# Two quads' sums joined between VectorE's block transpositions, their rows in another order as the output weights are loaded

## The chip, the cores and the metric

The kernel runs on one core of a Trainium2 chip. A core has a matrix engine (TensorE, in the profile PE, with its weight loads as PEld), a vector engine (VectorE, DVE), an engine for functions such as exp (ScalarE, ACT), a general engine (GpSimd, POOL) and an engine that issues transfers (SyncE, SP). Every engine has a queue of its own, works through it in order, and waits on semaphores of the others. All transfers of this kernel are issued from SP's queue, and 16 DMA engines carry them.

The metric is the device time of one execution in microseconds (us); lower is better. A difference of some 0.2% is about what can be told from no change.

## What is computed

Four attention layers stand one behind the other on x of 2048 tokens by 512 features. Layers 0 and 2 (kind A) look back over a window of 256 tokens; layers 1 and 3 (kind B) look at all tokens, with no causal mask. Both kinds have 32 heads of 16 features, with their own weights, and each kind's weights serve two layers.

```python
def _A_ref(x, wqkv, wo):
    B, S, D = x.shape
    H = 32; Dh = D // H; W = 256
    qkv = (x @ wqkv).reshape(B, S, 3, H, Dh).transpose(2, 0, 3, 1, 4)
    q, k, v = qkv[0], qkv[1], qkv[2]
    scores = jnp.einsum("bhqd,bhkd->bhqk", q, k) * (Dh ** -0.5)
    mask = (idx[:, None] - idx[None, :] >= 0) & (idx[:, None] - idx[None, :] < W)
    scores = jnp.where(mask[None, None], scores, -1e9)
    p = _softmax(scores, axis=-1)
    o = jnp.einsum("bhqk,bhkd->bhqd", p, v)
    return o.transpose(0, 2, 1, 3).reshape(B, S, D) @ wo
...
x = x + _A_ref(_layernorm(x, axis=-1), A_wqkv, A_wo)
x = x + _B_ref(_layernorm(x, axis=-1), B_wqkv, B_wo)
x = x + _A_ref(_layernorm(x, axis=-1), A_wqkv, A_wo)
x = x + _B_ref(_layernorm(x, axis=-1), B_wqkv, B_wo)
```

## The kernel before

**Tiles and loops.** The 2048 queries go in four chunks of 512 (index c). The 32 heads go in eight quads of four heads (index qd); two quads make one of four head tiles of 128 features (t = qd // 2, and u = qd % 2 is the half). For each chunk and quad TensorE makes scores (`exps`, lines 693 to 706), ScalarE takes exp of them (line 705), in the windowed layers GpSimd zeroes the edges of the window (lines 768 and 771), and TensorE multiplies with the values into one PSUM bank `a` (line 745 in the full layers, 778 in the windowed ones). Head h of the quad stands in partitions 32h to 32h+16: 16 rows of sums and one row with the sum of the weights.

**The epilogue of a quad (lines 664 to 690).** VectorE transposes the bank in blocks of 32 by 32 (line 671), so that queries are in the partitions and the 32 rows of a head side by side; takes the sums of weights, records their least and their total (674, 675), makes reciprocals (677, 678) and multiplies the 16 sums (679). It transposes back (681) into `o`, where half of the 32 rows of each head mean nothing. It then splits `o` into a float16 part (683) and the float16 rest (684, on GpSimd in layers 1 and 3 except for the last quad), into the tile `hl`. Four transfers (line 688) take the 16 good rows of each head from `hl` into the packed tile `O[l, c, t]`, 64u + 16h + d being the row. `o` and `hl` have one buffer each, O has five.

**The output projection.** `wo` (627) and, in layer 3, `wo_part` (646) multiply O with the output weights on TensorE (lines 415 and 418, as "oh" in the profile), scale columns with `gcol`, add to x and write it back to a scratch tensor. `ONR[l, c, t]` holds the modelled time at which O is taken to be there: 9 us after the epilogue is written out.

**Weights.** `prep` does the preparation of one matrix beside other work: `load_w` (270) loads it in one transfer of 1 MB with row k\*128 + p in partition p, `maxima` takes the columns' maxima, `scales` (303) makes powers of two from them, and `parts` (325) makes two float16 parts, which go to a scratch tensor `wd` (347) and are loaded from there by each projection (383, 385). The scales of the values' columns (`upv`) are multiplied onto the rows of the output weights (line 280).

**What sets the order.** TensorE's order is written out by hand. While a layer's attention runs, `Side` puts pieces of "works" (projections K, Q, VV for the next chunk or layer, and OO, the output projection) between its steps; a piece comes when a modelled clock says that what it needs is there (`DONE`, `ONR`) and by a share of the steps. A planner orders the other engines' queues; in the full layers the epilogue's first transposition is put ahead. SP's queue carries, in one order, the loads of queries and keys of each quad (`qt`, lines 718 and 731; `kt`, 722, 732 and 734), of weights, of x, the transposing transfers of the normalised x (`xc<-xh`, 476), the writes of projections, and the four transfers of line 688.

**The end.** The last thing is the part of layer 3's output projection that uses the last two quads; only then x goes out.

Of the kernel before, what the change touches and what calls it, by code (L numbers as in the profile page):

```python
# [9 lines left out]
F32 = mybir.dt.float32  # L10
BF16 = mybir.dt.bfloat16
F16 = mybir.dt.float16
# [3 lines left out]
ALU = mybir.AluOpType  # L16
AX = mybir.AxisListType

S, D, H, DH, WIN = 2048, 512, 32, 16, 256
P = 128  # L20
# [3 lines left out]
NHT = H // HT  # L24
QC = 512
NQ = S // QC
EPS = 1e-5
NQD = H // 4
# [5 lines left out]
EB, XB, XNB, WB, VB, OB = 6, 4, 4, 2, 3, 5  # L34
# [141 lines left out]
def interleave_kernel(tc, *args):  # L176
    nc = tc.nc
    with tc.tile_pool(name="flag", bufs=1) as fp:
        flag = fp.tile([1, 1], I32, name="flag")
        fast_path(tc, flag, *args)  # L180
        good = nc.values_load(flag, min_val=0, max_val=P)
        with tc.If(good < P):
            general_path(tc, *args)
# [3 lines left out]
def fast_path(ctx, tc, flag, a_x, a_wqkv, a_wo, b_wqkv, b_wo, out):  # L187
# [3 lines left out]
    nc = tc.nc  # L191
    pool = lambda name, bufs, **k: ctx.enter_context(tc.tile_pool(name=name, bufs=bufs, **k))
    cp = pool("const", 1)
    wp = pool("wts", 2)
    vp = pool("work", 2)
# [9 lines left out]
    mats = {(ty, s): layers[ty][1][:, s * D:(s + 1) * D] if s < 3 else layers[ty][2]  # L205
            for ty in range(2) for s in range(4)}

    XC, XN, V, O, KM, PH = {}, {}, {}, {}, {}, {"free": 0.0}
    CM, DN, DC, WT, ST, pend = {}, {}, {}, {}, {}, []

    clock, DONE, XNR, ONR = [0.0], {}, {}, {}
# [11 lines left out]
    acc = [ps_c.tile([P, QC], F32, name=f"acc{i}") for i in range(2)]  # L223
    turn = {"s": 0, "bank": 0}
    ident = cp.tile([P, P], F32, name="ident")
    onesf = cp.tile([P, P], F32, name="onesf")
    ones = cp.tile([P, QC], F16, name="ones")
    hsum = cp.tile([P, 32], BF16, name="hsum")
    es = cp.tile([P, 2, 2, NHT], F32, name="es")
    upv = cp.tile([P, 2, NHT], F32, name="upv")  # L230
# [10 lines left out]
    rows = lambda t: t.rearrange("p (h r) n -> (p h) r n", r=R)  # L241

    make_identity(nc, ident)
    nc.gpsimd.memset(onesf, 1.0)
    nc.gpsimd.memset(ones, 1.0)
    nc.gpsimd.memset(zeros, 0.0)
# [22 lines left out]

    def load_w(ty, s):  # L270
        raw = wp.tile([P, NC, D], F32, name=f"wr{ty}_{s}", tag="vf", bufs=NQ)
        nc.sync.dma_start(raw, mats[ty, s].rearrange("(k p) f -> p k f", p=P))
        return raw

    def maxima(ty, s, raw):
# [27 lines left out]
    def scales(ty, s):  # L303

        n = f"{ty}_{s}"
        cm = CM.pop((ty, s))
        up = es[:, ty, s, :] if s < 2 else upv[:, ty, :] if s == 2 else vp.tile([P, NHT], F32, name=f"wu{n}", tag="wc", bufs=8)
        dn = vp.tile([P, NHT], F32, name=f"wn{n}", tag="wc", bufs=8)
        nc.vector.tensor_scalar(up.bitcast(I32), cm.bitcast(I32), 0x7F800000, None, op0=ALU.bitwise_and)
        nc.vector.tensor_scalar(dn.bitcast(I32), up.bitcast(I32), -1, 0x7F000000, op0=ALU.mult, op1=ALU.add)  # L310
        DC[ty, s] = dn
        for v, name in ((up, "u"), (dn, "d"))[0 if s == 3 else 1:]:
            dg = vp.tile([P, NHT, P], F32, name=f"{name}g{n}", tag="oe")
            nc.vector.tensor_tensor(dg, ident[:, None, :].broadcast_to([P, NHT, P]),
                                    v[:, :, None].broadcast_to([P, NHT, P]), ALU.mult)
            yield
            pb = bank()
            nc.tensor.matmul(pb, onesf, dg.rearrange("p t f -> p (t f)"), start=True, stop=True)
            if name == "u":
                nc.vector.tensor_copy(gcol[ty], pb)  # L320
            else:
                DN[ty, s] = vp.tile([P, D], F32, name=f"wd{n}", tag="dn", bufs=2)
                nc.scalar.activation(DN[ty, s], pb, AF.Copy)

    def parts(ty, s, raw, act):

        dnb = DN.pop((ty, s))
        w = wp.tile([P, NC, 2, D], F16, name=f"w{ty}_{s}", tag="vf", bufs=NQ)
        hi, lo = w[:, :, 0, :], w[:, :, 1, :]
        mul = lambda k: (nc.vector if act else nc.gpsimd).tensor_tensor(raw[:, k, :], raw[:, k, :], dnb, ALU.mult)  # L330
        cast = lambda k: nc.scalar.activation(hi[:, k, :], raw[:, k, :], AF.Copy)
        rest = lambda k: nc.gpsimd.tensor_tensor(lo[:, k, :], raw[:, k, :], hi[:, k, :], ALU.subtract)
        if act:
            for k in range(NC):
                mul(k), cast(k), rest(k)
                yield
            WT[ty, s] = w
        else:

            for f, n, pause in (mul, 1, 2), (cast, 2, 1), (rest, 1, 0):  # L340
                for k in range(NC):
                    f(k)
                    if k % n == n - 1:
                        yield
                for _ in range(pause):
                    yield
        nc.sync.dma_start(wd[ty, s], w)

    def prep(ty, s):
        raw = load_w(ty, s)  # L350
        yield wait(14)
        for _ in maxima(ty, s, raw):
            yield wait(2)
        yield -spent(1.0)
        for _ in scales(ty, s):
            yield wait(4)
        if (ty, s) == (1, 0):
            share(1)
        yield -spent(0.5)
        for _ in parts(ty, s, raw, False):  # L360
            yield wait(2)
# [34 lines left out]
    def bank():  # L396

        if PH["full"]:
            return acc[1]
        turn["bank"] += 1  # L400
        if turn["bank"] % 2 and not PH["win"]:
            return ps_s.tile([P, 2, QC], F32, name=f"bs{turn['bank']}", tag="s")[:, 0, :]
        return PH["pool"].tile([P, QC], F32, name=f"b{turn['bank']}", tag="b")
# [260 lines left out]
    def epilogue(l, c, qd, a):  # L664


        n = f"{l}_{c}_{qd}"
        t, u = divmod(qd, 2)
        ot = vp.tile([P, QC // 32, 32], F32, name=f"ot{n}", tag="oe")
        with tc.high_priority(HEAD_START if l % 2 else 0):  # L670
            nc.vector.transpose(ot.rearrange("p b r -> p (b r)"), a)  # L671
        den = ot[:, :, DH]

        nc.vector.tensor_tensor(lmin, lmin, den, ALU.min)
        nc.vector.tensor_add(lsum, lsum, den)
        r = vp.tile([P, QC // 32], F32, name=f"r{n}", tag="r")
        nc.vector.tensor_scalar_max(r, den, L_MIN)
        nc.vector.reciprocal(r, r)
        nc.vector.tensor_tensor(ot[:, :, :DH], ot[:, :, :DH], r[:, :, None].broadcast_to([P, QC // 32, DH]), ALU.mult)
        o = vp.tile([P, QC], F32, name=f"o{n}", tag="o", bufs=1)  # L680
        nc.vector.transpose(o, ot.rearrange("p b r -> p (b r)"))
        hl = vp.tile([P, 2, QC], F16, name=f"hl{n}", tag="hl", bufs=1)
        nc.vector.tensor_copy(hl[:, 0], o)  # L683
        (nc.gpsimd if l % 2 and (l, c, qd) != (3, NQ - 1, NQD - 1) else nc.vector).tensor_tensor(hl[:, 1], o, hl[:, 0], ALU.subtract)  # L684
        if u == 0:
            O[l, c, t] = wp.tile([P, 2, QC], F16, name=f"oh{n}", tag="ohl", bufs=OB)
        for h in range(4):
            nc.sync.dma_start(O[l, c, t][64 * u + DH * h:64 * u + DH * h + DH], hl[32 * h:32 * h + DH])  # L688
        if u:
            ONR[l, c, t] = clock[0] + 9  # L690


    def exps(name, kt, qt, pr, pieces):
# [248 lines left out]
    def attention(l, works):  # L942
# [5 lines left out]
        for t in range(NHT if l == 3 else 1):  # L948
            for c in range(NQ):
# [10 lines left out]
                for qd in qds:  # L960
                    if (l, c, qd) == (1, 0, NQD // 2):
                        sd.finish()
                        sd = Side(NT * NQD * NQ - NT * NQD // 2, works[1], works[2], 0.33)
                    nxt = load(l, c, qd + 1) if qd + 1 in qds else None
                    a = acc[qd % 2 if win else 0]
                    began = clock[0]
                    for f in (attn_win if win else attn_full)(l, c, qd, *ops, a):
                        clock[0] = max(clock[0], began + (2.4 if win else 1.8))
                        began = clock[0]
                        pvq.append([f])  # L970
                        flush(2)
                        sd.step()
                        if win:
                            settle(False)
                    pvq[-1].append(lambda l=l, c=c, qd=qd, a=a: epilogue(l, c, qd, a))
                    ops = nxt
# [55 lines left out]
    phase(None)  # L1032
    xs = load_x(0, 0)
    raw = {m: load_w(0, m) for m in (1, 0, 2)}
    fill(kw[0], True)
    fill(qs[0, 0], False)
# [6 lines left out]
    for i in range(4):  # L1043
# [4 lines left out]
        nc.scalar.activation(xT[:, :, i * P:(i + 1) * P], pt, AF.Copy)  # L1048
    first_maxima(1, raw[1], (2, 3))
    sck = scales(0, 1)  # L1050
    next(sck)
    first_maxima(0, raw[0], range(NHT))
    scq = scales(0, 0)
    next(scq)
    share(0)
# [123 lines left out]
```

## Time and profile before

| | us |
|---|---|
| median of 3 runs | 2828.33 |
| lowest, highest | 2823.97, 2830.4 |
| the profiled execution's own time | 2829.59 |
| its span in the profile | 2827.9 |
| PE busy | 2655.6 (94%) |
| ACT busy | 2374.9 (84%) |
| DVE busy | 1033.6 (37%) |
| POOL busy | 613.8 (22%) |

The profile is of one execution, whose time is 1.69 us longer than its span and 1.26 us longer than the median. The granted clock of TensorE is 0.985 on average. The span falls into stages: 0 to 85 us first loads and projections, 85 to 490 the attention of layer 0, to 555 the projections between, to 1500 layer 1, to 1805 the attention of layer 2, to 1862 the projections between, to 2800 layer 3, and 28 us of end.

In rows of groups, the first number behind the bar is the busy time in us, then the mean of one instruction in ns, then the idle time of the engine just before them and what ended it. In rows of time, the first number is the start and the second the length of the group, and brackets hold the idle time before it with what ended it. "SPq" is SP's queue: its rows are the issuing of transfers, not their flight.

### The profile page before, as it was taken

How to read it: one execution, taken by the hardware profiler on the slowest of the kernel's cores; microseconds unless marked ns; L12 is line 12 of the kernel's file. 1: busy time of each engine (PE TensorE's matmuls, PEld its weight loads, DVE VectorE, ACT ScalarE, POOL GpSimd, SP SyncE). 2: the span in 40 equal slices, each digit the busy share in tenths (PEclk: the TensorE clock that was granted, in tenths of full speed). 3: DMA queues.
4: the chain of work that ended last, by engine and by line, in shares of the span. 5: the costliest groups of instructions: out<-in, count | busy, mean ns of one | idle time of the engine just before them, and what ended most of it. 6: DMA issues, size and time to landing. Idle time of an engine off the chain costs nothing.

```text
span 2827.9 us, 59285 instructions
## 1 busy us (share of the span) xinstructions
PE 2655.6 (94%) x23538; PEld 764.4 (27%) x23538; DVE 1033.6 (37%) x2201; ACT 2374.9 (84%) x2703; POOL 613.8 (22%) x1160
## 2 busy tenths in 40 slices
PE   8888897999999999999998888989999999999997
PEld 4333343422222222222222333422222222222221
DVE  7677765311123123112326566712222322223222
ACT  3565565499999999999996666579999999999996
POOL 2476564000100000000014567400000000000000
PEclk9998999999999999999999999999999999999998
DMA  6766776622223223322324555543333333333331
GB/s 215 203 206 202 215 221 196 186 77 65 94 79 110 76 86 99 96 85 91 109 81 133 184 171 158 157 126 100 111 112 105 118 119 110 112 102 119 106 97 58
DMA packets 320864, 359.99 MB, mean 127 GB/s; under 512 B 120896, under 2 KB 227904, under 8 KB 313920
## 3 DMA queue, kind: packets, MB, share of 16 engines
q1 hardware_dynamic: 320576, 356.10, 41.4%
q8 instruction: 187, 3.06, 0.4%
q14 instruction: 101, 0.83, 0.1%
HBM read 226.49 MB, written 96.99 MB: 114 GB/s over the span
## 4 chain that ended last, share of the span: by engine, by line
PE 70%; ACT 10%; DVE 7%; issue 5%; DMA 4%; POOL 2%; SPq 1%; ACTq 0%; DVEq 0%
PE acc L745 29%; PE s L701 18%; ACT e L705 9%; PE b L418 9%; PE acc L415 9%; PE acc L778 3%; PE bs L418 2%; DVE ot L671 1%; DMA wv<-wd 1%; DMA kt<-kw 1%; DVE xh L455 1%; POOL e L771 1%; DMA qt<-qs 1%; SPq L688 1%; DVE sp L514 1%
## 5 line engine op out<-in xcount | busy, mean ns | idle before, releaser
L705 ACT ACTIVATE e<-s 128x1024 f32<-128x1024 f32 (+2 forms) x2432 | 2237.8, 1160 | 125.4 <-PE s L701 120.1
L745 PE MATMUL acc<-e,vt 128*17 128x512 f32 x8192 | 1078.0, 598 | 4.6 <-DVE ot L671 3.2
L701 PE MATMUL s<-qt,kt 64*128 64x512 f16 (+3 forms) x5504 | 791.9, 356 | 91.3 <-ACT e L705 33.2
L701 PEld LDWEIGHTS <-kt 64*128 64x128 f16 x5504 | 213.0, 94 | 904.2 <-issue 844.0
L684 POOL TENSOR_TENSOR hl<-o,hl 128x512 f16<-128x512 f32 x63 | 73.1, 1160 | 1076.1 <-DVE hl L683 953.4
L671 DVE STREAM_TRANSPOSE ot<-acc 128x512 f32<-128x512 f32 x128 | 91.3, 713 | 554.9 <-PE acc L745 484.2
L771 POOL TENSOR_SCALAR_AFFINE_SELECT e<-e 128x256 f32<-128x256 f32 x512 | 233.0, 462 | 133.4 <-ACT e L705 133.0
L745 PEld LDWEIGHTS acc<-e,vt 128*17 128x17 f32 x8192 | 136.2, 95 | 359.9 <-issue 328.8
L768 POOL TENSOR_SCALAR_AFFINE_SELECT e<-e 128x256 f32<-128x256 f32 x448 | 203.3, 459 | 109.5 <-ACT e L705 108.3
L778 PE MATMUL acc<-e,vt 128*17 128x384 f32 (+2 forms) x2816 | 207.7, 399 | 3.7 <-POOL e L768 3.6
L418 PE MATMUL b<-xc,w 128*128 128x512 f16 x684 | 164.0, 392 | 23.3 <-DMA w<-wd 16.3
L511 ACT ACTIVATE sp<-b,es 128x512 f16<-128x512 f32 x57 | 39.1, 686 | 111.7 <-PE b L418 104.9
L519 POOL TENSOR_TENSOR sq_h<-sp_h 128x512 bf16<-128x512 f16 x27 | 28.9, 1072 | 450.7 <-DVE sp_h L513 450.7
L513 DVE TENSOR_SCALAR sp<-acc,es 128x512 f16<-128x512 f32 x28 | 21.0, 749 | 271.7 <-PE acc L415 271.7
L415 PE MATMUL acc<-xc,w_h 128*32 128x512 f16 x1296 | 114.5, 379 | 2.3 <-DVE km L552 2.3
L415 PE MATMUL acc<-xc,w 128*32 128x512 f16 x1344 | 108.7, 379 | 0.1
L659 DVE TENSOR_TENSOR dx<-acc,gcol 128x512 f32<-128x512 f32 x60 | 41.5, 692 | 178.8 <-PE acc L415 178.8
L415 PE MATMUL acc<-wo,oh 128*32 128x512 f16 x1296 | 102.1, 379 | 0.7 <-DVE m L564 0.7
L418 PEld LDWEIGHTS <-w 128*128 128x128 f16 x720 | 68.3, 100 | 123.7 <-issue 36.7
L622 ACT ACTIVATE vt<-b 128x256 f32<-128x256 f32 (+1 forms) x50 | 21.1, 450 | 93.1 <-PE b L418 93.1
L513 DVE TENSOR_SCALAR sp_h<-acc,es 128x512 f16<-128x512 f32 x27 | 19.9, 738 | 217.0 <-PE acc L415 206.7
L418 PE MATMUL b<-wo,oh 128*128 128x512 f16 x390 | 93.8, 391 | 4.8 <-DMA wo<-wd 4.8
(166 smaller groups left out, 1787.4 us busy)
## 6 DMA issues: line engine op xcount, KB each, us to landing
kt<-kf SPq DMA_DIRECT2D x128, 512.0 KB
qt<-qs SPq DMA_DIRECT2D x128, 256.0 KB
xd<-x SPq DMA_DIRECT2D x96, 256.0 KB
x<-xd SPq DMA_DIRECT2D x96, 256.0 KB
w<-wd SPq DMA_DIRECT2D x20, 1024.0 KB
kt<-kw SPq DMA_DIRECT2D x64, 256.0 KB
oh<-hl SPq DMA_DIRECT2D x512, 32.0 KB
qs<-sp SPq DMA_DIRECT2D x48, 256.0 KB
```

The costliest lines, as they stand in the source:

```text
L415: nc.tensor.matmul(ps[g:g + 32], a[:, g:g + 32], b, start=(i == 0), stop=(i == len(pairs) - 1), skip_group_check=True)
L418: nc.tensor.matmul(ps, a, b, start=(i == 0), stop=(i == len(pairs) - 1))
L513: nc.vector.tensor_scalar(sp[:, 0], ps, e, None, op0=ALU.mult)
L659: nc.vector.tensor_tensor(d, ps, gcol[1], ALU.mult)
L671: nc.vector.transpose(ot.rearrange("p b r -> p (b r)"), a)
L684: (nc.gpsimd if l % 2 and (l, c, qd) != (3, NQ - 1, NQD - 1) else nc.vector).tensor_tensor(hl[:, 1], o, hl[:, 0], ALU.subtract)
L701: nc.tensor.matmul(ps[:, h, s0:s0 + wd_], kt[R * h:R * h + R, pr, kc:kc + P], qt[R * h:R * h + R, pr, qc:qc + wd_], start=True, stop=True)
L705: nc.scalar.activation(e[:, :, w0:w1], ps[:, :, w0:w1], AF.Exp, scale=SCALE)
L745: nc.tensor.matmul(a[32 * h:32 * h + DH + 1, :], V[l, qd // 4, j // 8][:, j % 8, 4 * (qd % 4) + h, :], es_[h // 2][:, h % 2, :], start=(j ...
L768: nc.gpsimd.affine_select(v, v, pattern=[[0, 2], [-1, P]], compare_op=ALU.is_gt, fill=0.0, base=0, channel_multiplier=1)
L771: nc.gpsimd.affine_select(v, v, pattern=[[0, 2], [1, P]], compare_op=ALU.is_ge, fill=0.0, base=0, channel_multiplier=-1)
L778: nc.tensor.matmul(a[32 * h:32 * h + DH + 1, q * P:(q + nb) * P], V[l, (4 * c + j) // 4][:, j % 4, 4 * qd + h, :], es_[h // 2][:, h % 2, s ...
```

## The change

The sums of quad u are multiplied with the reciprocals into half of a joint tile `OT[t]`, whose 32 rows are u, then d. Only at the second quad of a head tile is this transposed back, once for both; the result has all 128 rows in use, row 32h + 16u + d. The split into two float16 parts is written directly into O, and the transfers of line 688 are gone. O's buffer is taken at the second quad, and the modelled time until O is there is 4.5 us in place of 9.

The rows of O are so in another order within each head tile. The output weights' rows are loaded in this order, in eight transfers of 16 partitions (128 KB each) in place of one, and the scales of the values' columns, which are multiplied onto these rows, are brought into it by a TensorE product with a permuted identity, which GpSimd makes once at the start, and a VectorE copy, once for each kind of layer.

```diff
+    perm = cp.tile([P, P], F32, name="perm")
...
+    nc.gpsimd.tensor_copy(perm.rearrange("p (h u d) -> p u h d", u=2, d=DH), ident.rearrange("p (u h d) -> p u h d", u=2, d=DH))
...
     def load_w(ty, s):
         raw = wp.tile([P, NC, D], F32, name=f"wr{ty}_{s}", tag="vf", bufs=NQ)
-        nc.sync.dma_start(raw, mats[ty, s].rearrange("(k p) f -> p k f", p=P))
+        if s < 3:
+            nc.sync.dma_start(raw, mats[ty, s].rearrange("(k p) f -> p k f", p=P))
+        else:
+
+            for u in range(2):
+                for h in range(4):
+                    nc.sync.dma_start(raw[32 * h + DH * u:32 * h + DH * u + DH],
+                                      mats[ty, s].rearrange("(k u h d) f -> u h d k f", u=2, h=4, d=DH)[u, h])
         return raw
...
-        up = es[:, ty, s, :] if s < 2 else upv[:, ty, :] if s == 2 else vp.tile([P, NHT], F32, name=f"wu{n}", tag="wc", bufs=8)
+        up = es[:, ty, s, :] if s < 2 else vp.tile([P, NHT], F32, name=f"wu{n}", tag="wc", bufs=8)
...
+        if s == 2:
+
+            pu = bank()
+            nc.tensor.matmul(pu[:, :NHT], perm, up, start=True, stop=True)
+            nc.vector.tensor_copy(upv[:, ty, :], pu[:, :NHT])
...
         nc.vector.reciprocal(r, r)
-        nc.vector.tensor_tensor(ot[:, :, :DH], ot[:, :, :DH], r[:, :, None].broadcast_to([P, QC // 32, DH]), ALU.mult)
-        o = vp.tile([P, QC], F32, name=f"o{n}", tag="o", bufs=1)
-        nc.vector.transpose(o, ot.rearrange("p b r -> p (b r)"))
-        hl = vp.tile([P, 2, QC], F16, name=f"hl{n}", tag="hl", bufs=1)
-        nc.vector.tensor_copy(hl[:, 0], o)
-        (nc.gpsimd if l % 2 and (l, c, qd) != (3, NQ - 1, NQD - 1) else nc.vector).tensor_tensor(hl[:, 1], o, hl[:, 0], ALU.subtract)
         if u == 0:
-            O[l, c, t] = wp.tile([P, 2, QC], F16, name=f"oh{n}", tag="ohl", bufs=OB)
-        for h in range(4):
-            nc.sync.dma_start(O[l, c, t][64 * u + DH * h:64 * u + DH * h + DH], hl[32 * h:32 * h + DH])
+            OT[t] = vp.tile([P, QC // 32, 2, DH], F32, name=f"op{n}", tag="op", bufs=1)
+        nc.vector.tensor_tensor(OT[t][:, :, u, :], ot[:, :, :DH], r[:, :, None].broadcast_to([P, QC // 32, DH]), ALU.mult)
         if u:
-            ONR[l, c, t] = clock[0] + 9
+            o = vp.tile([P, QC], F32, name=f"o{n}", tag="o", bufs=1)
+            nc.vector.transpose(o, OT.pop(t).rearrange("p b u d -> p (b u d)"))
+            hl = O[l, c, t] = wp.tile([P, 2, QC], F16, name=f"oh{n}", tag="ohl", bufs=OB)
+            nc.vector.tensor_copy(hl[:, 0], o)
+            (nc.gpsimd if l % 2 and (l, c, qd) != (3, NQ - 1, NQD - 1) else nc.vector).tensor_tensor(hl[:, 1], o, hl[:, 0], ALU.subtract)
+            ONR[l, c, t] = clock[0] + 4.5
```

More of the change, by code (lines that the diff above doesn't have):

```diff
@@ L206, in fast_path @@
             for ty in range(2) for s in range(4)}
-    XC, XN, V, O, KM, PH = {}, {}, {}, {}, {}, {"free": 0.0}
+    XC, XN, V, O, OT, KM, PH = {}, {}, {}, {}, {}, {}, {"free": 0.0}
     CM, DN, DC, WT, ST, pend = {}, {}, {}, {}, {}, []
```

## The prediction

> **What bounds the kernel now.** I read the page's head first, then a table of busy time by stage (stretch, its length, then busy us and instructions of PE, PEld, DVE, ACT and POOL, the granted clock, the DMA share and GB/s).
>
> ```profile
> span 2827.9 us, 59285 instructions
> ```
>
> ```profile
> 85.00:490.00 405.00, 343.63 (x2902) 136.83 (x2902) 268.95 (x544) 229.32 (x297) 243.64 (x504) 0.94 0.70 210
> ...
> 555.00:1500.00 945.00, 933.58 (x8988) 217.79 (x8984) 198.84 (x453) 941.96 (x1020) 65.98 (x62) 1.00 0.28 87
> 1500.00:1805.00 305.00, 262.41 (x2614) 103.64 (x2606) 209.38 (x465) 192.50 (x234) 206.35 (x479) 0.98 0.57 169
> ...
> 1862.00:2800.00 938.00, 921.74 (x8148) 218.84 (x8150) 231.32 (x455) 934.34 (x1021) 64.58 (x58) 1.00 0.34 105
> ```
>
> The full layers (945 and 938 us) belong to ScalarE's exps: it is idle 945.0 - 942.0 = 3.0 us in layer 1 and 938.0 - 934.3 = 3.7 us in layer 3. The change touches no exp, so these two stages can give at most 6.7 us, and I expect none of it. The windowed layers are another case: no engine is full, and TensorE, whose order is fixed by hand, stands idle for 405.0 - 343.6 = 61.4 us and 305.0 - 262.4 = 42.6 us. So I read next what TensorE waits for there (layer 0 first, then layer 2), and what SP's queue waits for in the same two stretches.
>
> ```profile
> PE s L701 <- DMA kt<-kw: 18.3, 5, 6.6
> PE b L418 <- DMA w<-wd: 16.3, 2, 12.7
> PE s L701 <- ACT e L705: 6.4, 15, 1.0
> ```
>
> ```profile
> PE s L701 <- ACT e L705: 24.0, 46, 1.1
> PE s L701 <- DMA qt<-qs: 8.8, 3, 5.6
> PE s L701 <- DMA kt<-kw: 7.5, 1, 7.5
> ```
>
> ```profile
> SPq L688 <- DVE hl L684: 76.5, 23, 12.1
> ...
> SPq L688 <- DVE hl L684: 41.2, 24, 6.0
> ```
>
> About half of the idle time ends with a transfer: 18.3 + 16.3 = 34.6 us and 8.8 + 7.5 = 16.3 us, 50.9 in all. And the queue that issues all transfers stands for 76.5 + 41.2 = 117.7 us at line 688, waiting for VectorE's rest, with the loads behind it. That is what the change takes away.
>
> **The change part by part.** The groups that it halves or removes:
>
> ```profile
> L681 DVE STREAM_TRANSPOSE o<-ot 128x512 f32<-128x512 f32 x128 | 90.9, 710 | 8.6 <-DVE ot L679 0.5
> L683 DVE CAST hl<-o 128x512 f16<-128x512 f32 x128 | 58.8, 459 | 14.8 <-DMA oh<-hl 11.5
> L684 DVE TENSOR_TENSOR hl<-o,hl 128x512 f16<-128x512 f32 x65 | 52.6, 809 | 1.5
> ```
>
> ```profile
> L688 SPq DMA_DIRECT2D oh<-hl x512: 507/582/2464, 88.4 to 2812.9; - x171
> ```
>
> *VectorE.* Each pair of quads saves one transposition, one cast and one rest: 0.71 + 0.46 + 0.81 = 1.98 us, 16 pairs in each windowed layer, so about 32 us a layer of 269 and 209 busy. VectorE is busy 66 to 69% there and is not the bound: I count nothing for it by itself. In the full layers VectorE is busy a fifth to a quarter of the time, and the exps hide all of it. The multiply (679) and the first transposition stay as they are.
>
> *SP's queue.* 512 issues of 0.58 us are 298 us, half of them in the windowed layers (149 us of their 710), and its standing at line 688 goes as well. What this is worth is read at the five longest waits behind it, each with its rows. **A**, layer 0:
>
> ```profile
> 253.15 0.53 SPq L731 DMA_DIRECT2D qt<-qs  x1
> 258.57 2.42 SPq L688 DMA_DIRECT2D oh<-hl  x4
> 261.04 0.58 SPq L732 DMA_DIRECT2D kt<-kw  x1
> ```
>
> ```profile
> 264.42 1.04 PE L701 MATMUL s<-qt,kt 64*128 64x128 f16 x8 [6.62 <-DMA kt<-kw]
> ```
>
> The queue stands from 253.68, issues the four and only then the keys. Without them the keys go up to 7.3 us earlier: the whole 6.62 goes, if their buffer is free by then. **B**:
>
> ```profile
> 336.59 0.47 SPq L272 DMA_DIRECT2D wr<-in_B_wo_dram  x1
> ...
> 338.83 3.01 SPq L688 DMA_DIRECT2D oh<-hl  x4
> 341.94 0.52 SPq L383 DMA_DIRECT2D w<-wd  x1
> ```
>
> ```profile
> 349.46 5.30 PE L418 MATMUL b<-xc,w 128*128 128x512 f16 x12 [3.56 <-DMA w<-wd]
> ```
>
> Without the four the weights go 3.1 us earlier: 3.1. (The load at 336.59 is one that the change splits; that is priced below.) **C**, the longest:
>
> ```profile
> 429.64 0.77 DVE L455 TENSOR_TENSOR xh<-xn,xh 128x512 f16<-128x512 f32 x1
> ```
>
> ```profile
> 435.20 2.41 SPq L688 DMA_DIRECT2D oh<-hl  x4
> 437.66 2.69 SPq L476 DMA_TRANSPOSE xc<-xh  x2
> 440.45 0.52 SPq L383 DMA_DIRECT2D w<-wd  x1
> ```
>
> ```profile
> 446.09 7.77 PE L418 MATMUL b<-xc,w 128*128 128x512 f16 x24 [12.73 <-DMA w<-wd]
> ```
>
> The transposing transfers' data are there at 430.4, but they are issued at 437.66 behind the four, and the weights behind them: 7.2 us. **D** and **E**, layer 2:
>
> ```profile
> 1551.99 2.41 SPq L688 DMA_DIRECT2D oh<-hl  x4
> 1554.50 0.53 SPq L731 DMA_DIRECT2D qt<-qs  x1
> ```
>
> ```profile
> 1557.39 0.82 PE L701 MATMUL s<-qt,kt 64*128 64x384 f16 x4 [5.59 <-DMA qt<-qs]
> ```
>
> ```profile
> 1650.78 0.39 SPq L731 DMA_DIRECT2D qt<-qs  x1
> 1652.79 2.43 SPq L688 DMA_DIRECT2D oh<-hl  x4
> ...
> 1656.41 0.44 SPq L732 DMA_DIRECT2D kt<-kw  x1
> ```
>
> ```profile
> 1659.90 1.03 PE L701 MATMUL s<-qt,kt 64*128 64x128 f16 x8 [7.48 <-DMA kt<-kw]
> ```
>
> D gives 2.5 us (1551.99 to 1554.50). In E the queue stands from 1651.17 to 1655.22: 4.1 us. Together A to E: 6.6 + 3.1 + 7.2 + 2.5 + 4.1 = 23.5 us.
>
> *Slow matmuls behind a wait.* In B twelve products behind 3.56 us of idleness take 5.30 us, and elsewhere as many take 2.76:
>
> ```profile
> 1566.31 2.76 PE L418 MATMUL b<-xc,w 128*128 128x512 f16 x12
> ```
>
> So B loses 5.30 - 2.76 = 2.5 us more, and C 7.77 - 5.52 = 2.2; for A, D and E I take 1 us each, an estimate between nothing and B's. That is 7.7; since C, D and E only shrink, I count half: 4 us. The Trainium skill ("TensorE: Matmul & The Clock Gate", "What's actually happening") says that the array's clock is halved after an idle window of about 3.4 us and is whole again after a busy one; B's 3.56 us and its doubled time agree. By that rule A's loss goes with its wait, B's goes only if its wait falls below that window, and C's, with 5 us still idle, stays: 1 to 3.5 in place of 4.
>
> *The end.*
>
> ```profile
> 2810.34 0.69 DVE L684 TENSOR_TENSOR hl<-o,hl 128x512 f16<-128x512 f32 x1
> ```
>
> ```profile
> 2814.97 1.44 PE L418 MATMUL bs<-wo,oh 128*128 128x512 f16 x3 [7.88 <-DMA oh<-hl]
> ```
>
> Nothing covers the last four transfers: 2814.97 - 2811.03 = 3.9 us. They go, and everything behind moves up with them. This is the one term that I take whole.
>
> *What is added.* The eight-part load puts 7 more issues of 0.58 us, 4.1 us, before the loads behind it, twice. One of the two places is B, where they eat the 3.1 us that the four give back. At the other, some 100 us into the span, two groups of four (2.4 us each) go from ahead of it. From both sides the two cost between nothing and 8.1 us; I take 4, the one of B. The Trainium skill ("DMA: Bandwidth & Descriptors", "Rules for kernel authors") advises against splitting a load by partitions, and its "Anatomy of one DMA" gives each transfer a fixed cost of about 2.0 us. Paid one after the other, eight would take an estimated 16 us; the end's four took 3.9 us from first issue to use, which speaks against paying in turn. The permuting product, its copy and GpSimd's copy come once or twice, on engines with idle time in those stages; the nearest rows bound each by a cast (0.46 us) and nothing: nothing. The product itself stands in TensorE's queue, but its operand is older than the one of the product ahead of it, so it adds no wait. VectorE now waits for a free O buffer at the cast, where SP waited before; the epilogues queued behind it would wait with it. Five buffers are as many as before and are taken a quad later: nothing.
>
> *The earlier due time.* TensorE's output products are placed up to 4.5 us earlier. By the means above, two transpositions, the cast and the rest take 2 x 0.71 + 0.46 + 0.81 = 2.7 us, which leaves 1.8 for the epilogue's five small steps: 4.5 holds when VectorE comes at once. I count nothing, and put the case where it doesn't among the rivals.
>
> *The sum.* Queue 23.5 and clock 4 make 27.5. A load that lands earlier may meet the next wait (the exps end 46 waits in layer 2 alone), so I take three quarters, 20.6; with the end 3.9 and the split load +4 that is -20.5. From the profiled execution's 2829.59 it gives 2809.1; this execution is 1.26 above the median of the runs, 2828.33, so the forecast is 2807.8: **2808 us**.
>
> **The rivals.**
> - *Only the end is won.* The loads would be held by something else than line 688, such as buffers that TensorE has not yet freed. For it: only the stalls' neighbours in the queue show the cause, not a buffer's state. Against: in A and E the queue stands with nothing else ahead. 3.9 against 4: **2828**; within 0.2% (2822.7 to 2834.0).
> - *Part of it.* Half of A to E and no clock: 11.8 + 3.9 - 4 = 11.7, **2817**.
> - *More.* All 50.9 us of waits on transfers go with 7.7 of slow products and the end: -62 at the most. Half of the waits that are not in A to E (50.9 - 36.0 = 14.9) on top of my terms in full, 23.5 + 7.7 + 7.5 + 3.9 = 42.6, with the split load hidden: **2786**.
> - *Slower: the output products come too early.* TensorE works in order, so a product placed before its sums are there stops all scores behind it. In C a layer norm keeps VectorE busy until 430.4 ahead of an epilogue; seven output projections in and between the windowed layers could meet such a row, at 6.0 us each, the longest that SP's queue stood for a rest in layer 2: +42, against my -20.5: **2850**. It decides from 2.9 us a place (20.5 / 7) on. Against: three of the seven stand behind a key projection, and in the waits above TensorE waits for no sums in either layer.
>
> **How the numbers follow.** Chances: the forecast (2795 to 2813) 0.57, part of it (2813 to 2822.7) 0.20, more (under 2795) 0.10, only the end 0.08, slower 0.05. Faster by over 0.2% is 0.57 + 0.20 + 0.10 = 0.87, same 0.08, slower 0.05. A difference of 0.2% is about what a measurement of this kernel can tell from no change. The range 2786 to 2822 leaves out "only the end", "slower" and the far half of "more", some 0.18. It takes in both ends of the split load's cost.
>
> **What would show it.** In the profile of the changed kernel no `oh<-hl` is issued, and the waits of `s` on `kt` and `qt` and of `b` on `w` in the windowed stages fall from 50.9 to some 30 us, while these stages shorten by about 17 us together and the full layers by under 2. The last product follows the last rest within 0.2 us. VectorE's busy time falls by some 101 us (64 of each of 681 and 683, 32 of VectorE's 684). If the windowed stages keep their length although SP's queue no longer stands, a buffer held the loads; if `wo,oh` products wait for VectorE, the due time is wrong. I would be most wrong if the planner, with other times, orders VectorE's queue otherwise, since stalls of this size come and go with that order.

## The result and the profile after

| | before | after |
|---|---|---|
| median, us | 2828.51 (2823.97 to 2830.4, 4 runs) | 2776.06 (2775.41 to 2777.61, 4 runs) |
| span of the profiled execution, us | 2827.9 | 2774.5 |
| layer 0, first to last product with the values | 418.6 | 381.9 |
| layer 2, the same | 298.1 | 285.0 |
| layer 1, from its first product with the values to layer 2's first | 955.2 | 956.6 |
| layer 3, from layer 2's last product with the values to layer 3's last | 999.1 | 997.1 |
| the end, from the last product with the values | 21.4 | 17.8 |

The ratio is 0.9818, 95% interval 0.9801 to 0.9835: 1.8% faster, and 10 us below the lower end of the range. Of the span's 53.4 us, 36.7 come from layer 0, 13.1 from layer 2, 3.6 from the end; the full layers stay as they were (+1.4 and -2.0), and so do the projections between layers 0 and 1 (65.7 to 65.4).

First the table of stages, cut at the first and last product with the values of each windowed layer: before, then after. The columns are those of the prediction's table.

```profile
69.80:488.40 418.60, 355.93 (x2984) 140.93 (x2986) 281.11 (x573) 237.12 (x309) 253.38 (x526) 0.94 0.70 211
...
1509.30:1807.40 298.10, 254.78 (x2556) 100.62 (x2554) 206.63 (x458) 189.23 (x228) 204.31 (x475) 0.98 0.57 169
```

```profile
70.70:452.60 381.90, 346.92 (x2986) 139.68 (x2988) 259.95 (x526) 236.59 (x309) 248.30 (x526) 0.97 0.75 220
...
1474.60:1759.60 285.00, 252.59 (x2554) 100.51 (x2554) 178.29 (x411) 188.84 (x228) 196.12 (x475) 0.99 0.57 165
```

TensorE's idle time falls from 62.7 to 35.0 us in layer 0 and from 43.3 to 32.4 in layer 2. Its busy time falls too, by 9.0 and 2.2 us, with nearly the same number of products (two more in layer 0, two fewer in layer 2); the granted clock rises from 0.94 to 0.97 and from 0.98 to 0.99.

What TensorE waits for in the two stages after the change, layer 0 and then layer 2 (in all, times, longest):

```profile
PE s L714 <- ACT e L718: 11.1, 23, 1.2
PE b L432 <- DMA w<-wd: 7.4, 1, 7.4
PE b L432 <- DVE sp L528: 6.9, 6, 2.4
PE acc L791 <- POOL e L781: 4.4, 6, 1.4
PE s L714 <- DMA kt<-kw: 1.9, 1, 1.9
```

```profile
PE s L714 <- ACT e L718: 25.7, 49, 1.1
PE s L714 <- DMA qt<-qs: 3.7, 1, 3.7
```

Three waits on transfers are left, 7.4 + 1.9 + 3.7 = 13.0 us. Before there were thirteen, 57.7 us in the same stages (the prediction's 50.9 and two more kinds that it did not add, `wo` 4.8 and `wv` 2.0). What came in their place is small: the waits on exps, the largest, grow from 30.4 (6.4 + 24.0) to 36.8 us.

SP's queue in layer 0 now stands for other things; its longest rows after the change:

```profile
SPq L538 <- ACT sp L525: 40.0, 16, 6.4
SPq L744 <- PE s L714: 28.5, 12, 8.1
SPq L654 <- DVE x L653: 28.1, 11, 7.3
SPq L539 <- DVE sp L528: 24.6, 15, 5.3
```

It still stands, but it is earlier in its order: at line 744 it waits for TensorE to leave the buffer of `qt`, which is to say that the queries are as early as their two buffers let them be.

The end, in order of time. The first product no longer waits for any transfer:

```profile
2760.10 0.43 DVE L701 CAST oh<-o 128x512 f16<-128x512 f32 x1
2760.56 0.69 DVE L702 TENSOR_TENSOR oh<-o,oh 128x512 f16<-128x512 f32 x1
...
2760.59 1.46 PE L432 MATMUL bs<-wo,oh 128*128 128x512 f16 x3 [3.27 <-DVE oh L701]
```

It starts right behind the cast, and beside the rest, since the first two of its terms use the first float16 part alone.

### The profile page after: what moved, and what is told of

Its sections match the earlier page's. It is cut to its first block, busy times and chain, and to the rows that moved or that the text cites. A ratio compares the mean times of both kernels' runs of the same rounds, so it can differ in the third digit from the quotient of the medians.

```text
span 2774.5 us, 58038 instructions
## 1 busy us (share of the span) xinstructions
PE 2643.8 (95%) x23542; PEld 764.6 (28%) x23542; DVE 949.8 (34%) x2043; ACT 2374.8 (86%) x2703; POOL 563.4 (20%) x1129
## 4 chain that ended last, share of the span: by engine, by line
PE 72%; ACT 11%; issue 6%; DVE 5%; DMA 3%; POOL 3%; SPq 0%; ACTq 0%; DVEq 0%; POOLq 0%
PE acc L758 29%; PE s L714 19%; PE b L432 10%; ACT e L718 10%; PE acc L429 9%; PE acc L791 3%; PE bs L432 2%; DVE ot L686 1%; POOL e L784 1%; POOL wr L344 1%; POOL e L781 1%; DVE sp L528 1%; DMA kt<-kw 0%; DMA x<-in_A_x_dram 0%; POOL w L346 0%
## 5 line engine op out<-in xcount | busy, mean ns | idle before, releaser
L784 POOL TENSOR_SCALAR_AFFINE_SELECT e<-e 128x256 f32<-128x256 f32 x512 | 228.8, 454 | 125.8 <-ACT e L718 125.6
L702 POOL TENSOR_TENSOR oh<-o,oh 128x512 f16<-128x512 f32 x31 | 35.9, 1159 | 909.1 <-DVE oh L701 909.1
L781 POOL TENSOR_SCALAR_AFFINE_SELECT e<-e 128x256 f32<-128x256 f32 x448 | 194.6, 440 | 96.1 <-ACT e L718 94.4
L533 POOL TENSOR_TENSOR sq<-sp 128x512 bf16<-128x512 f16 x28 | 29.1, 1039 | 396.9 <-DVE sp L527 396.9
```

Source lines behind the costliest of these rows:

```text
L533: nc.gpsimd.tensor_tensor(sq, sp[:, 0], sp[:, 0], ALU.mult)
L781: nc.gpsimd.affine_select(v, v, pattern=[[0, 2], [-1, P]], compare_op=ALU.is_gt, fill=0.0, base=0, channel_multiplier=1)
L784: nc.gpsimd.affine_select(v, v, pattern=[[0, 2], [1, P]], compare_op=ALU.is_ge, fill=0.0, base=0, channel_multiplier=-1)
```

## The experiments

Two theories stood at the beginning. **Queue**: the four transfers of each quad, by their issue and by standing for VectorE's rest, hold the loads behind them in SP's queue. **VectorE**: the halved transpositions, casts and rests shorten the chains. The times beside which each is read are 2776 for the change and some 2826 for the kernel before (2825.8 to 2826.7 in the sets below).

**The transfers left out, VectorE's work kept.** This is the kernel before with:

```diff
-        hl = vp.tile([P, 2, QC], F16, name=f"hl{n}", tag="hl", bufs=1)
+        if u:
+            hl = O[l, c, t] = wp.tile([P, 2, QC], F16, name=f"oh{n}", tag="ohl", bufs=OB)
+        else:
+            hl = vp.tile([P, 2, QC], F16, name=f"hl{n}", tag="hl", bufs=1)
...
-        if u == 0:
-            O[l, c, t] = wp.tile([P, 2, QC], F16, name=f"oh{n}", tag="ohl", bufs=OB)
-        for h in range(4):
-            nc.sync.dma_start(O[l, c, t][64 * u + DH * h:64 * u + DH * h + DH], hl[32 * h:32 * h + DH])
```

It leaves out the first quad of each pair, so its output is not the reference's; every engine but SP does its work of before.

> The kernel before with only its sums' transfers left out: VectorE still transposes, casts and subtracts for every quad, and the due time stays at 9 us; the output product so leaves out the first quad of each pair and mixes rows. Theory 'queue' (the transfers of sums hold the loads behind them in SP's queue): nearly the whole gain, 2776 to 2788 us, the excess over 2776 being VectorE's extra work. Rival 'VectorE' (the halved transpositions, casts and rests shorten the chains): 2815 to 2828 us, little more than the 3.6 us of the end is won.

2773.89 us (2773.11 to 2778.01), ratio 0.9819 (0.9802 to 0.9836): the whole gain, to within the measurement. So the halved VectorE work is worth nothing that can be told, and "VectorE" falls.

**The same transfers, back in the kernel before's places, with nobody behind them but the queue.** The run before, plus (in `epilogue`, for every quad; `spare` is a scratch tensor in device memory that nobody reads):

```diff
+        for h in range(4):
+            nc.sync.dma_start(spare[t][64 * u + DH * h:64 * u + DH * h + DH], hl[32 * h:32 * h + DH])
```

> The kernel before with its four transfers a quad at their place, behind the same waits for VectorE's rest, but to a scratch tensor that nobody reads; the second quad's two parts are written into O directly (the output leaves out the first quad of each pair). SP's queue is as full and stands as often as before; only the output product no longer waits for a landing. Theory 'queue, standing included': 2812 to 2824 us, all but the end is lost again. If the landing in the output product's own path was a part of the gain: 2795 to 2810 us.

2821.73 us (2815.63 to 2824.42), ratio 0.9984 (0.9974 to 0.9993). All is lost again but some 4 us, which is the end: it takes 17.5 us, where the kernel before took 21.4. The output products do not read what these transfers write, so it was not the sums' own way that cost the time. In this run TensorE waits as before the change, 51.8 us for transfers in the two windowed stages against 57.7. The longest of these waits, over the whole span:

```profile
PE s L703 <- DMA kt<-kw: 18.6, 7, 7.1
PE b L419 <- DMA w<-wd: 16.2, 2, 12.0
...
PE s L703 <- DMA qt<-qs: 9.3, 3, 4.8
PE b L419 <- DMA wo<-wd: 6.7, 1, 6.7
```

**The same transfers with nothing to wait for.** The same four transfers a quad, from a constant tile (`ones[32 * h:32 * h + DH, None, :].broadcast_to([DH, 2, QC])` in place of `hl[32 * h:32 * h + DH]`):

> The same with the four transfers of each quad from a constant tile: issued at the same places, with no wait for VectorE. Theory 'queue': the issuing alone costs what the eight idle transfers a pair cost, 2785 to 2798 us, and the difference to the run before it is the price of standing. If order and place matter rather than standing: within 5 us of that run.

2786.83 us (2784.74 to 2791.22), ratio 0.9863 (0.9848 to 0.9878). The transfers and their bytes are as many as in the run before, but their places are others than the expectation says. With nothing to wait for, all 512 go out by 837.2 us, 128 of them in layer 0 and none in layer 2. The first row is of this run, the other two are of the run before, where they go out all along the span:

```profile
L690 SPq DMA_DIRECT2D spare<-ones x512: 547/590/3001, 81.0 to 837.2; - x171
```

```profile
L690 SPq DMA_DIRECT2D spare<-hl x256: 302/412/2059, 88.7 to 2782.8; - x128
L690 SPq DMA_DIRECT2D spare<-oh x256: 303/414/1880, 95.8 to 2810.3; - x128
```

So 2786.83 - 2773.89 = 12.9 us is what the 512 cost at these other places, and 2821.73 - 2786.83 = 34.9 us is not the price of standing alone: it also holds all that the transfers cost in layer 2.

**The same question on the changed kernel**, with eight transfers at each second quad, from constants and from the packed tile:

```diff
+            for k in range(8):
+                nc.sync.dma_start(spare[t][DH * k:DH * k + DH], ones[DH * k:DH * k + DH, None, :].broadcast_to([DH, 2, QC]))
```

> The changed kernel plus eight transfers of 32 KB at each second quad, from a constant tile to a scratch tensor that nobody reads: as many issues as before (512), but none waits for VectorE. If the issuing time (0.58 us each, 149 us in the windowed layers) is what held the loads: 2795 to 2815 us. If it was the queue's standing for VectorE's rest (118 us): 2776 to 2785 us. Rival 'VectorE': 2776 to 2779 us.

> The same eight transfers at each second quad, now from the packed tile itself, so that SP's queue stands until VectorE's (or GpSimd's) rest is done; nobody reads what they write. Theory 'queue': most of the loss is back, 2800 to 2824 us, and it lies in the windowed layers as waits of TensorE on kt, qt and w. Rival 'VectorE': 2776 to 2782 us, since VectorE's work is that of the changed kernel.

From constants: 2793.52 us (2786.64 to 2796.87), ratio 0.9889 (0.9872 to 0.9906). From the tile (`hl[DH * k:DH * k + DH]`): 2802.18 us (2800.96 to 2805.58), ratio 0.992 (0.9903 to 0.9936). VectorE does the change's work in both, and with the waiting transfers half of the gain is gone all the same. Why the other half stays, these runs do not tell: the queue stands once a pair in place of twice, and VectorE's work is halved too. The transfers from constants have again moved: 123 of them are issued in layer 0, none in layer 2. The profiled executions of these two runs and of the three before them tell where the time goes (us, first to last product with the values):

| | layer 0 | layer 2 |
|---|---|---|
| no transfers | 382.4 | 282.6 |
| four a quad, constants | 399.1 | 281.8 |
| four a quad, waiting | 415.1 | 299.4 |
| eight a pair, constants | 396.2 | 282.7 |
| eight a pair, waiting | 395.8 | 295.6 |

Only layer 0 has about as many of the transfers in all four runs that have any. There 128 transfers that wait for nothing cost 399.1 - 382.4 = 16.7 us, and waiting, four a quad, costs 16.0 more; eight a pair, waiting costs nothing more (395.8 against 396.2). In layer 2 the runs from constants have no such transfers, so the 17.6 and 12.9 us there are issuing and standing together. These are single executions, up to 6.9 us from their run's median (the eight from constants). What issuing and standing cost apart, at the same places, is therefore not shown; in layer 0 they come out about equal.

**The small parts.** The due time of 9 us in the changed kernel (`ONR[l, c, t] = clock[0] + 9`):

> The changed kernel with the modelled time until the sums are there back at 9 us from 4.5. Theory 'queue': within 4 us of 2776. Rival 'due time' (earlier placed output products fill TensorE's idle time): 2785 us or more.

2772.9 us (2771.59 to 2774.29), which looked like a gain of 3 us, so it was run again beside the changed kernel:

> The changed kernel with the due time of 9 us, beside the changed kernel on the same chip: if the earlier due time costs something of itself, 2 to 4 us less than the changed kernel; if the two differed by chance, within 1 us.

> The changed kernel itself on the same chip as the run before: 2774 to 2778 us.

2775.71 us (2772.4 to 2776.83) and, for the changed kernel, 2773.82 (2771.17 to 2776.09), so the order of the two turned round. The due time makes no difference that can be told.

The weights' load in one piece (line 272's first branch for every matrix):

> The changed kernel with the output weights loaded in one transfer as before, so that their rows are in another order than the sums (the output is not the reference's). If the eight-part load costs the 4 us that the prediction gave it: 2772 us. If it is hidden: within 2 us of 2776.

2775.89 us (2772.18 to 2777.77), ratio 0.9823 (0.981 to 0.9836): the eight-part load costs nothing that can be told. (In this run the rows of the output weights are in another order than the sums, so the output is not the reference's.)

**The transfers on another queue.** The kernel before with `nc.gpsimd.dma_start` in place of `nc.sync.dma_start` at line 688:

> The kernel before with nothing changed but the queue that issues the four transfers: GpSimd's in place of SP's. Theory 'queue': SP's loads are as free as in the changed kernel, 2780 to 2805 us, less than the full gain since GpSimd's queue also zeroes the window's edges and now stands for VectorE's rest. Rival (that standing and issuing on GpSimd holds the edges and so TensorE): 2826 us or more. Theory 'VectorE': 2820 to 2830 us.

2860.58 us (2855.17 to 2869.69), ratio 1.013 (1.0107 to 1.0154): slower than before by 34.8 us, as the rival named ahead had it. SP's loads are free: in the two windowed stages TensorE's waits on `kt`, `qt`, `w`, `wo` and `wv` fall from 57.7 us to 1.0, though the same bytes move, which speaks for the queue and against the transfers' traffic as what held the loads (TensorE's longer waits for other things give the loads time, too). But now GpSimd stands. Its own group of issues, and below it what TensorE waits for:

```profile
L688 POOL DMA_DIRECT2D oh<-hl x512 | 252.8, 498 | 188.8 <-DVE hl L684 139.0 <-POOL hl L684 17.8 <-issue 10.2
```

```profile
PE s L701 <- ACT e L705: 42.0, 76, 1.7
PE acc L778 <- POOL e L768: 33.6, 21, 5.9
...
PE b L418 <- DMA oh<-hl: 9.6, 3, 4.5
```

The products with the values wait 33.6 us for the window's edges, 2.8 + 0.7 before, because the edges stand behind the transfers in GpSimd's queue:

```profile
240.37 1.93 POOL L688 DMA_DIRECT2D oh<-hl  x4 [6.56 <-DVE z L46]
242.30 0.42 POOL L771 TENSOR_SCALAR_AFFINE_SELECT e<-e 128x256 f32<-128x256 f32 x1
```

GpSimd is idle for 6.56 us there, with the edge of line 771 next in order. VectorE is held as well: its casts wait 72.3 us for the transfers to leave `hl`, where they waited 11.5 before. Layer 0 comes out even (417.9 against 418.6 us) and layer 2 is 22.8 us longer (320.9 against 298.1). The same transfers, moved to a queue with other work behind them, cost more than where they were; the runs do not part GpSimd's edges from VectorE's casts in this.

## Why the prediction was right and wrong

**Right: the bound and the mechanism.** The full layers gave nothing, the windowed ones all but the end, through waits on loads behind line 688. The rival "only the end is won", in which buffers would have held the loads, did not come; the queue now stands for TensorE's reading of a buffer (line 744), but early enough for the loads to be in time. "Slower" did not come either: no output product waited for its sums before the end.

**Right in size: the end and the parts at nothing.** 3.9 us were taken and 3.6 measured. VectorE's saving, the permuting product and the due time were taken at nothing and are nothing that can be told. The three groups of VectorE that were to fall by 101 us fell by 98.0, its busy time as a whole by 83.8. Only the permuted scales' copy shows, as one wait of TensorE of 0.9 us for `upv` in layer 0, where the prediction expected none.

**Wrong: the term "queue", 23.5 us and three quarters of it.** This is the step that failed. The waits on transfers fell by 57.7 - 13.0 = 44.7 us, where 17.6 were taken. The fault is the eight waits outside A to E: the sum took them at nothing and gave no reason. They were 57.7 - 36.0 = 21.7 us, three of them (4.8, 4.2 and 3.8 us) longer than B's 3.56, and after the change one is left, of 1.9 us on `kt`: 19.8 us that the forecast did not have. One of the eight, in the kernel before:

```profile
324.92 2.41 SPq L688 DMA_DIRECT2D oh<-hl  x4
...
335.46 0.50 SPq L732 DMA_DIRECT2D kt<-kw  x1
336.01 0.54 SPq L734 DMA_DIRECT2D kt<-kw  x1
```

```profile
340.07 0.61 PE L701 MATMUL s<-qt,kt 64*128 64x128 f16 x8 [2.71 <-DMA kt<-kw]
```

No group of four stands right ahead of these keys, the last one before them ends 8.1 us earlier, and yet the wait went with the groups. The reading that fits is that a queue that works in order carries its lateness on: a load is late by what all earlier groups have cost and what the queue could not make up since. The runs show that the waits come and go with the groups; they do not follow one load's lateness back through the queue.

The five waits that the prediction did price came out at 24.8 us against 23.5, but partly by luck, since the errors of its neighbour-by-neighbour prices cancel: A, B and E are gone whole (6.62, 3.56 and 7.48, where 6.6, 3.1 and 4.1 were given), while D went from 5.59 to 3.74 (1.9, where 2.5 was given) and C from 12.73 to 7.40 (5.3, where 7.2 was given). C after the change:

```profile
400.34 1.23 SPq L490 DMA_TRANSPOSE xc<-xh  x1
401.67 0.52 SPq L397 DMA_DIRECT2D w<-wd  x1
```

```profile
410.41 7.65 PE L432 MATMUL b<-xc,w 128*128 128x512 f16 x24 [7.40 <-DMA w<-wd]
```

No group of four is ahead of the weights any more, but their landing takes 8.7 us, from 401.67 to 410.36, where it took 5.6 before (440.45 to 446.04).

The discount of a quarter, for "the next wait", was 6.9 us. What came back was 6.1: 44.7 us of waits and 11.2 of busy time went, and the two stages became shorter by 49.8. In us that is close, but as a share it is a ninth, since twice as much went.

**Wrong in size: the slow products.** 4 us were taken, 3 after the discount; TensorE's busy time in the two stages fell by 9.0 + 2.2 = 11.2, while the granted clock rose. In C the 24 products behind 7.4 us of idleness still take 7.65 us. The Trainium skill's rule ("TensorE: Matmul & The Clock Gate", "What's actually happening"), by which an idle window of about 3.4 us halves the clock, agrees: C's loss stayed with its wait. The prediction counted slow products behind five waits; they stood behind others too, such as this one of 5.30 - 2.76 = 2.5 us in the kernel before:

```profile
213.64 5.30 PE L418 MATMUL b<-wo,oh 128*128 128x512 f16 x12 [4.81 <-DMA wo<-wd]
```

**Wrong: the split load at +4.** It is nothing that can be told. That the queue now has time for seven more issues fits this, but no run shows it. The fixed cost of about 2.0 us that the prediction quoted is given by the Trainium skill ("DMA: Bandwidth & Descriptors", "Anatomy of one DMA") for transfers that GpSimd issues, and the eight go from SP's queue; no run here times it for them.

**The miss, added up.** The two windowed stages were to become 20.6 - 4 = 16.6 us shorter and became 49.8 shorter. Of the 33.2 us between, 19.8 are the eight waits, 7.2 the slow products, 4 the split load, 1.3 A to E and 0.8 the discount.

**The rival "more"** had the right picture, and its bound for all transfers, 50.9 + 7.7 + 3.9 = 62.5 us, holds the measured 52. Its own 2786 was worked out with half of the other waits, and the range ended at it, too high by 10 us. A range that took in the bounds would have reached 2766.

## What to carry to other kernels

An engine's queue that issues transfers should be read as a resource. A group of transfers in it that waits for a producer makes the loads behind it late by its issuing and by the time that the queue stands for it; in layer 0 here the two cost about the same, 16.7 and 16.0 us, in one execution each. When such groups are removed, take all waits on loads in that stage as the term, less a little, and not only the waits right behind a group. Moving a waiting transfer to another engine's queue moves the stand; what is behind it there decides. A control that takes a wait away can also move the work that waited: find in its trace where that work went before reading its time as the price of the wait.

## What was not expected of the hardware

Transfers that wait for nothing are not free in a busy queue: 128 of 32 KB each made layer 0 longer by 16.7 us (399.1 against 382.4), while the 384 others of that run went out from there to 837.2 us, and all that lies outside layers 0 and 2 became longer by only 1.1 us. GpSimd issued the same transfers in 498 ns each on the mean, SP in 582 at the median.
